# Beacon attention and a max-of-three feed-forward layer on one core: full-height arrays for the first batch's third key tile, the beacon keys and the pairs cast on the chip

## The chip, the cores and the metric

The kernel runs on one core of a Trainium2 chip. The metric is device time in microseconds of one execution. Engines are named as the profile names them: PE is TensorE (matmuls), PEld its weight loads, DVE is VectorE, ACT is ScalarE, POOL is GpSimd, SP is SyncE, which here only issues transfers.

## The reference

Causal attention over 8 batches of 8 heads, with 576 tokens of width 64 and 16 beacon keys and values ahead of them that every token sees; its output, laid out as 4608 tokens by 512, goes through three matrices of 512 by 768, of which the elementwise maximum is taken, and a fourth of 768 by 512.

```python
k_all = np.concatenate([beacon_k, k], axis=2)          # 16 + 576 keys
v_all = np.concatenate([beacon_v, v], axis=2)
scores = scale * np.matmul(q, k_all.transpose(0, 1, 3, 2))
scores = np.where(causal, -1000000000.0, scores)       # beacons are never masked
a = np.exp(scores - scores.max(-1, keepdims=True))
a /= a.sum(-1, keepdims=True) + 1e-09
x = np.matmul(a, v_all)                                # then (B, S, H*D) -> (4608, 512)
h = np.maximum(np.maximum(x @ w1, x @ w2), x @ w3)
return (h @ w_out).astype(np.float32)
```

## The kernel before, in words

Heads are worked in pairs (two heads of 64 fill 128 partitions); four pairs make a batch, two pairs a "quad", 32 pairs in all. For each pair the queries and keys are brought to the layout width by token (`qT`, `kT`), the beacon keys standing ahead of the keys in `kT`, so that there are 592 keys in five tiles of 128, 128, 128, 128 and 80 rows. `emit_scores` (L506) computes scores with keys on the partitions, in four groups per pair, each 64 rows of contraction by 128 columns; ScalarE takes the exponential of a group at once (L532); the triangle is then masked by VectorE (L549, a product with a triangle) or GpSimd (L551). `emit_pv` (L571) multiplies by the values: for a quad and a token half it makes four passes over the key tiles, the first with a block of ones (the sums), the others with the even and odd columns of the values, each matmul 32 columns wide, four of them side by side in the array. `invert_sums` (L606, ScalarE: logarithm and exponential) and `multiply` (L618, VectorE) write the normalized output as `xT`, and the feed-forward units read it: first the three matrices and their maximum (L643 and L666), then the fourth (L685).

Batch 0 is worked in two token halves of 288 (`HALF`), so that the work can begin when half the tokens of a pair have come. In its first half the third key tile holds only 48 keys that any of these tokens sees (`K2`, L97): 16 beacons and 288 tokens less 256. `rows_of` (L99) gives 48 there and the whole tile's rows elsewhere; the value matmuls (L585), the view of the exponentials (L497) and the masks (L542) all go by it. `kT` is set to zero beyond the first half's keys at the start (L151), so the exponentials of the other 80 rows exist.

How the first pairs come in: for pairs 0 and 1, first half, fp32 transfers (`load_half`, L210) are cast on the chip (`cast_half`, L218) into a tile of 96 rows by head, row, width; pairs 2 and 3 and all second halves come cast by the transfer itself (`load_quad`, L226). `turn_half` (L431) turns them on TensorE: for each of the three row groups two transposes of 64 columns, one per head, at column positions 0 and 64. Ahead of each it can put `fill` transposes (L407) of a constant tile. `turn_beacons` (L344) turns the beacon keys: batch 0's with 16 rows, batches 1 to 3 with 48 rows, four transposes each. Later batches' pairs are cast by row, head, width (`cast_piece`, L245) and turned by full transposes of 128 columns (L401), or come back turned from memory.

The order of the work in batch 0 and most of batch 1 is written out by hand, one step after another (`first_steps`, L892 to L1067); each engine takes its instructions in that order. It begins:

```python
("load half", 0, 0, "sp"), ("busy", 17), ("identity",), ("busy", 8), ("triangle",),
...
("half", 0, 0, "ffn", "act", 0, 7),
("cast half", 1, 1, "act"),
("turn keys 0",),
```

"busy" are filler matmuls of 320 columns on the constant tile `busy` (L481), which the third memset from the top of the kernel's code writes on VectorE (L139); the last two numbers of a "half" step are fills ahead of the keys' and of the queries' transposes. The weights of the first layer are loaded by GpSimd's queue at three steps ("load w"), the second of which stands behind the mask of pair 0's second group; w_out is loaded behind a VectorE memset (L332).

Of the kernel before, what the change touches and what calls it, by code (L numbers as in the profile page):

```python
# [8 lines left out]
FP32 = mybir.dt.float32  # L9
BF16 = mybir.dt.bfloat16  # L10
# [6 lines left out]
def kernel(  # L17
# [13 lines left out]
    nc = tc.nc  # L31

    B, H, S, D = q.shape
    Nb = beacon_k.shape[2]
# [13 lines left out]
    QP = S // QR  # L48
    HR = QR // 2
# [160 lines left out]
    def load_half(p, i, queue):  # L210
        st = half_pool.tile([QP, 2, HR, D], FP32, name=f"h32{i}")
        queue.dma_start(
            out=st.rearrange("p h r d -> p h (r d)"),
            in_=half_source(p // PPQ, 0, i, 2 * (p % PPQ), 2),
        )
        stage["half", p, i] = st

    def cast_half(p, i, cast):  # L218
        t16 = half_pool.tile([QP, 2, HR, D], BF16, name=f"h16{i}")
        cast(  # L220
            t16.rearrange("p h r d -> p (h r d)"),
            stage.pop(("half", p, i)).rearrange("p h r d -> p (h r d)"),
        )
        stage["half16", p, 0, i] = t16

    def load_quad(g, h):  # L226
        for i in range(2):
# [115 lines left out]

    def turn_beacons(b0, b1, src):  # L344
        n = Nb * (b1 - b0)
        ps = sc_psum.tile([128, PPB, n], BF16, name="sc")
        for pi in range(PPB):
            nc.tensor.transpose(
                ps[:, pi],
                src[:, 2 * pi : 2 * pi + 2].rearrange("p h d -> p (h d)"),  # L350
                ident[0:n, 0:n],
            )
        if b0 == 0:
            by_act(kTs[0][:, 0:Nb], ps[:, 0, 0:Nb])
        by_act(bT[:, :, Nb * b0 : Nb * b1], ps)
# [48 lines left out]
                ident[0:QP, 0:QP],  # L404
            )

    def fill(ps, n):  # L407
        for i in range(n):
            x0 = 512 + QP * (i % 5)
            for e in range(2):  # L410
                nc.tensor.transpose(
                    ps[64 * e : 64 * e + 64, x0 : x0 + QP],
                    busy[0:QP, 0:64],
                    ident[0:QP, 0:QP],
                    tile_position=(0, 64 * e),
                )

    def keep_turning(n):
        ps = pv_bank(1, [128, 512], FP32)
# [11 lines left out]
    def turn_half(p, h, pv, q_copy=None, idle=0, idle_q=0):  # L431
        for i in range(2):
            src = stage.pop(("half16", p, h, i))
            if pv:
                bank = pv_bank(i, [128, 1024], BF16)
            else:
                bank = ffn_psum.tile([128, 1024], BF16, name="fps")
            ps = bank[:, 0:HALF]

            fill(bank, idle if i == 1 else idle_q)  # L440
            for r in range(HR):
                for e in range(2):
                    nc.tensor.transpose(
                        ps[64 * e : 64 * e + 64, r * QP : (r + 1) * QP],
                        src[:, e, r],
                        ident[0:QP, 0:QP],
                        tile_position=(0, 64 * e),
                    )
# [89 lines left out]
    def emit_masks(p, gi, dve=False):  # L538
        masked.add((p, gi))
        off = 0  # L540
        for t, q0, q1 in groups(p)[gi]:
            n = rows_of(p, t, q1)  # L542
            lo, hi = max(q0, k_tok[t]), min(q1, k_tok[t] + n)
            if lo < hi:
                view = both_heads(p, gi)[0:n, :, off + lo - q0 : off + hi - q0]
                x0 = lo - k_tok[t]
                if dve:
                    m = tri[0:n, None, x0 : x0 + hi - lo]
                    nc.vector.tensor_mul(view, view, m.to_broadcast([n, 2, hi - lo]))  # L549
                else:  # L550
                    nc.gpsimd.affine_select(  # L551
                        out=view,
                        in_=view,
                        compare_op=ALU.is_ge,
                        fill=0.0,
                        base=x0,
                        pattern=[[0, 2], [1, hi - lo]],
                        channel_multiplier=-1,
                    )
            off += q1 - q0  # L560
# [10 lines left out]
    def emit_pv(quad, hf, first=0, last=len(passes), banks=None):  # L571
        b, g = divmod(quad, n_quad)
        v_sb = v_tiles[b]
        for p in range(PPQ * quad, PPQ * (quad + 1)):
            assert all((p, gi) in masked for gi in range(1 if b == 0 and hf == 0 else NG))
        if first == 0:
            banks = banks or [pv_bank(i, [128, 512], FP32) for i in range(2)]
            pv_tiles[quad, hf] = banks
        ps = pv_tiles[quad, hf]
        for part, bank, lo, ca, cb in passes[first:last]:  # L580
            qa, qb = hf * HALF + ca, hf * HALF + cb
            ts = [t for t in range(n_kt) if q_min[t] < qb]
            for t in ts:
                q0 = max(qa, q_min[t])
                n = rows_of(PPQ * quad, t, qb)  # L585
                for j in range(4):
                    lhsT = (
                        ones[0:n]
                        if part == 0
                        else v_sb[0:n, t, head(g, j), part - 1 : D : 2]  # L590
                    )
                    nc.tensor.matmul(  # L592
                        ps[bank][32 * j : 32 * j + 32, lo + q0 - qa : lo + qb - qa],
                        lhsT,
                        at_view(PPQ * quad + j // 2, t, j % 2, q0, qb),
                        start=(t == 0),
                        stop=(t == ts[-1]),
                        tile_position=(0, 32 * j),
                    )
        if last == len(passes):  # L600
            unfinished.append((quad, hf))
# [246 lines left out]
    def widen():  # L848
# [17 lines left out]
        "cast half": lambda p, i, e: cast_half(p, i, by[e]),  # L866
        "cast keys 0": lambda e: by[e](bk16_0, bk32_0),
        "turn keys 0": lambda: turn_beacons(0, 1, bk16_0),
        "half": half,
        "whole": whole,  # L870
# [10 lines left out]
        "cast keys 1": lambda e: by[e](bk16_1, bk32_1),  # L881
        "cast pair": lambda p: cast_pair(p, by_pool, by_pool),
# [5 lines left out]
        "load pair": lambda p, gate="dve": load_pair(p, idle[gate]),  # L888
        "load": next_load,
        "store": lambda: store_y(len(y_out)),  # L890
    }
# [342 lines left out]
```

## Time and profile before

| what | value |
|---|---|
| median of 3 runs | 294.38 us (293.03 to 295.4) |
| profiled execution | 294.65 us, of which span 292.6 us |
| TensorE busy | 281.3 us, 3714 matmuls |
| VectorE, ScalarE, GpSimd busy | 169.6, 150.5, 115.8 us |
| moved by DMA | 49.50 MB, mean 169 GB/s |
| first value pass, first quad (L592) | 44 matmuls, 1.34 us of the chain from 14.60 us |
| first value pass, second quad (L592) | from 18.09 us |
| TensorE's longest waits | 1.3 us for the first memset, 0.7 for w_out, 0.6 for first-layer weights |

A line of a timeline has start and duration in us, engine, line of the kernel, operation, output and inputs by their names, the array shape as rows*columns, the shape of what streams, and how many instructions were merged; in brackets stands the idle time ahead of it and who ended it. The chain is the work that ended last, followed back from the last instruction, in order of time.

### The profile page before, as it was taken

The page shows a single profiled execution, that of the slowest core. Times are in us where ns is not written, and L with a number is a line of the kernel's source. Part 1 is how long each engine was busy: PE and PEld are TensorE (multiplying, and loading weights), DVE is VectorE, ACT ScalarE, POOL GpSimd, SP SyncE. Part 2 cuts the span into 40 slices and gives each one's busy share as a digit, 9 for nine tenths or more (in the row PEclk, how much of TensorE's full clock was granted, in tenths as well). Part 3 has the DMA queues.
Part 4 walks back from the last instruction along what each step waited for, and adds up shares of the span by engine and source line. Part 5 has one row for each costly group of instructions (what it writes and reads, how often), then busy time and mean ns, then how long its engine had stood idle before and what let it go on. Part 6 is the DMA issues. An engine that isn't in the chain of part 4 may idle for free.

```text
span 292.6 us, 8864 instructions
## 1 busy us (share of the span) xinstructions
PE 281.3 (96%) x3714; PEld 160.1 (55%) x3739; DVE 169.6 (58%) x319; ACT 150.5 (51%) x242; POOL 115.8 (40%) x238
## 2 busy tenths in 40 slices
PE   8889999989999999999999999999999999999995
PEld 4656677754454555454545887545454545444442
DVE  1555567837756575566655656565656564474273
ACT  3786576853566676846676256635663552200300
POOL 3618415742546583426454655466323420000000
PEclk9999999999999999999999999999999999999999
DMA  7999979999989999998999899999442003001103
GB/s 131 161 175 185 217 123 225 228 192 261 229 230 256 232 281 270 186 175 263 314 190 181 233 256 268 177 205 214 104 68 98 2 0 137 11 0 74 71 1 143
DMA packets 85111, 49.50 MB, mean 169 GB/s; under 512 B 64208, under 2 KB 79824, under 8 KB 85072
## 3 DMA queue, kind: packets, MB, share of 16 engines
q1 hardware_dynamic: 78864, 43.40, 66.6%
q0 software_dynamic: 5648, 5.21, 11.7%
q8 instruction: 29, 0.48, 0.7%
q10 hardware_dynamic: 560, 0.33, 0.4%
q14 instruction: 10, 0.08, 0.1%
HBM read 35.13 MB, written 14.22 MB: 169 GB/s over the span
## 4 chain that ended last, share of the span: by engine, by line
PE 86%; DMA 7%; POOL 2%; ACT 2%; DVE 1%; issue 1%; POOLq 0%
PE pv L654 21%; PE sc L654 15%; PE wide L654 8%; PE pv L690 6%; PE sc L690 6%; PE sc L517 5%; PE pv L592 4%; DMA w_out_sb<-in_moe_w_out_dram 4%; PE wide L690 3%; PE wide L592 3%; PE sc L592 3%; PE wide L517 3%; DMA w_sb<-in_moe_w_dram 3%; PE pv L481 2%; PE pv L673 1%
## 5 line engine op out<-in xcount | busy, mean ns | idle before, releaser
L532 ACT ACTIVATE at_sb<-sc 128x736 bf16<-128x736 f32 (+5 forms) x91 | 76.5, 867 | 59.3 <-PE sc L517 59.1
L551 POOL TENSOR_SCALAR_AFFINE_SELECT at_sb<-at_sb 128x256 bf16<-128x256 bf16 (+3 forms) x140 | 51.9, 387 | 117.3 <-ACT at_sb L532 117.1
L654 PEld LDWEIGHTS <-w_sb 128*128 128x128 bf16 x648 | 61.1, 98 | 60.4 <-issue 4.7
L654 PE MATMUL pv<-xT,w_sb 128*128 128x512 bf16 (+1 forms) x315 | 65.3, 347 | 0.3
L654 PE MATMUL sc<-xT,w_sb 128*128 128x512 bf16 (+1 forms) x205 | 45.6, 363 | 0.7 <-issue 0.2
L532 ACT ACTIVATE at_sb<-wide 128x736 bf16<-128x736 f32 (+3 forms) x37 | 31.3, 846 | 22.4 <-PE wide L517 22.4
L664 DVE TENSOR_TENSOR hT<-hT,pv 128x512 bf16<-128x512 bf16 x48 | 32.4, 686 | 13.0 <-PE pv L654 13.0
L690 PEld LDWEIGHTS <-hT 128*128 128x128 bf16 x210 | 19.6, 98 | 24.3 <-issue 1.1
L248 POOL CAST p<-st 96x768 bf16<-96x768 f32 x40 | 32.0, 824 | 0.0
L624 DVE TENSOR_TENSOR xT<-pv,recip 128x288 bf16<-128x288 f32 (+2 forms) x48 | 14.2, 350 | 26.7 <-ACT recip L614 26.7
L517 PE MATMUL sc<-qT,kT 64*128 64x288 bf16 (+6 forms) x290 | 27.2, 275 | 2.0 <-POOL at_sb L551 0.6
L664 DVE TENSOR_TENSOR hT<-hT,sc 128x1024 bf16<-128x1024 bf16 (+1 forms) x18 | 19.6, 1098 | 12.7 <-PE sc L654 12.5
L517 PEld LDWEIGHTS <-kT 64*128 64x128 bf16 x400 | 14.9, 94 | 21.8 <-issue 14.7
L592 PEld LDWEIGHTS <-v_sb 128*32 128x32 bf16 (+1 forms) x1408 | 24.7, 96 | 2.6 <-issue 1.3
L654 PE MATMUL wide<-xT,w_sb 128*128 128x512 bf16 (+1 forms) x110 | 24.5, 364 | 0.1
L690 PE MATMUL sc<-w_out_sb,hT 128*128 128x512 bf16 x79 | 19.1, 380 | 1.0 <-DMA w_out_sb<-in_moe_w_out_dram 0.7
L690 PE MATMUL pv<-w_out_sb,hT 128*128 128x512 bf16 x83 | 19.9, 380 | 0.1
L304 POOL CAST v_sb<-st 128x1536 bf16<-128x1536 f32 (+2 forms) x21 | 18.4, 895 | 0.0
L662 DVE CAST hT<-pv 128x512 bf16<-128x512 f32 x20 | 13.7, 688 | 4.8 <-PE pv L654 4.8
L673 PEld LDWEIGHTS <-w_sb 128*128 128x128 bf16 x144 | 13.1, 98 | 3.9 <-issue 1.4
L614 ACT ACTIVATE recip<-lnd 128x288 f32<-128x288 f32 x32 | 14.2, 444 | 1.0
L592 PEld LDWEIGHTS <-ones 128*32 128x32 bf16 (+2 forms) x512 | 11.0, 95 | 6.7 <-issue 4.7
(116 smaller groups left out, 286.3 us busy)
## 6 DMA issues: line engine op xcount, KB each, us to landing
st<-in_q_dram SPq DMA_DIRECT2D x24, 288.0 KB, 5.3
st<-in_k_dram SPq DMA_DIRECT2D x24, 288.0 KB, 5.7
st<-in_v_dram SPq DMA_DIRECT2D x24, 256.0 KB, 5.8
out_dram<-y SPq DMA_DIRECT2D x9, 512.0 KB, 3.3
out_dram<-y SPq DMA_DIRECT2D x17, 256.0 KB, 2.7
w_sb<-in_moe_w_dram POOLq DMA_DIRECT2D x6, 384.0 KB, 7.2
q_dram<-p SPq DMA_DIRECT2D x16, 144.0 KB, 3.1
k_dram<-p SPq DMA_DIRECT2D x16, 144.0 KB, 3.2
```

Source lines behind the costliest of these rows:

```text
L248: cast(t16.rearrange("p r h d -> p h r d"), st[0:QP, i * NQ2 : (i + 1) * NQ2].rearrange("p (h r d) -> p h r d", h=2, r=QR),)
L304: cast(v_sb[0:n, t:t1].rearrange("p t h d -> p (t h d)"), st[0:n, (t - t_lo) * H * D : (t1 - t_lo) * H * D],)
L517: nc.tensor.matmul(ps[:, e, off : off + q1 - q0], kT[hs, 128 * t : 128 * t + 128], qT[hs, q0:q1], start=True, stop=True, tile_position=(64 ...
L532: nc.scalar.activation(out=both_heads(p, gi), in_=ps[:, :, 0 : g_width(p, gi)], func=AF.Exp, scale=scale)
L551: nc.gpsimd.affine_select(out=view, in_=view, compare_op=ALU.is_ge, fill=0.0, base=x0, pattern=[[0, 2], [1, hi - lo]], channel_multiplier=-1,)
L592: nc.tensor.matmul(ps[bank][32 * j : 32 * j + 32, lo + q0 - qa : lo + qb - qa], lhsT, at_view(PPQ * quad + j // 2, t, j % 2, q0, qb), star ...
L614: nc.scalar.activation(out=recip, in_=lnd, func=AF.Exp, scale=-1.0)
L624: nc.vector.tensor_mul(xT[:, 2 * g + part - 1, c0 + ca : c0 + cb], ps[bank][:, lo : lo + cb - ca], recip[:, ca:cb],)
L654: nc.tensor.matmul(dst[:, o0 : o0 + n], w_in[i][:, ct, 128 * (ft + f) : 128 * (ft + f + 1)], xT[:, ct, x0 : x0 + n], start=(ct == 0), stop ...
L664: nc.vector.tensor_max(h, h, ps)
L673: nc.tensor.matmul(ps[:, f], w_in[i][:, ct, 128 * (ft + f) : 128 * (ft + f + 1)], xT[:, ct, tb * TOKB + lo : tb * TOKB + hi], start=(ct == 0),
L690: nc.tensor.matmul(ps[:, t - tt] if two else ps, hT[:, ft, 128 * t : 128 * (t + 1)], w_out_sb[:, ft, :], start=(ft == 0), stop=(ft == n_ft ...
```

## The change

Three things change; the written order of the steps stays as it is.

The function `rows_of` and `K2` go: in batch 0's first half the third key tile is multiplied, viewed and masked with all 128 rows. The beacon tiles `bk16_0` and `bk16_1` get 128 partitions and are set to zero by two memsets on VectorE, which stand ahead of the one for `busy`; their keys are turned by ordinary matmuls with the identity on 128 rows, into an fp32 bank. The casts of pairs 0 and 1, first half, write by row, head, width, and `turn_half` turns such tiles by one full transpose of 128 columns for each row group, with the fills ahead of them in the same form; tiles that come cast by the transfer are turned as before. A way to load half quads on other queues and some defaults of steps are added, and no step of the list uses them.

```diff
-    K2 = Nb + HALF - 256
-
-    def rows_of(p, t, q1):
-        return K2 if p < PPB and t == 2 and q1 <= HALF else k_rows[t]
...
-    bk16_0 = const.tile([Nb, H, D], BF16, name="bk16_0")
+    bk16_0 = const.tile([128, H, D], BF16, name="bk16_0")
+    nc.vector.memset(bk16_0, 0.0)
...
-    bk16_1 = const.tile([NB_PE - Nb, H, D], BF16, name="bk16_1")
+    bk16_1 = const.tile([128, H, D], BF16, name="bk16_1")
+    nc.vector.memset(bk16_1, 0.0)
...
+    def cast_half(p, i, cast, h=0):
+        t16 = half_pool.tile([QP, HR, 2, D], BF16, name=f"h16{i}")
+        cast(t16.rearrange("p r h d -> p h r d"), stage.pop(("half", p, h, i)))
...
-        ps = sc_psum.tile([128, PPB, n], BF16, name="sc")
+        ps = sc_psum.tile([128, PPB, n], FP32, name="sc")
         for pi in range(PPB):
-            nc.tensor.transpose(
+            nc.tensor.matmul(
                 ps[:, pi],
                 src[:, 2 * pi : 2 * pi + 2].rearrange("p h d -> p (h d)"),
-                ident[0:n, 0:n],
+                ident[:, 0:n],
+                start=True,
+                stop=True,
             )
...
+    def turn_column(dst, src, n):
+
+        if len(src.shape) == 2 and src.shape[1] == 128:
+            nc.tensor.transpose(dst, src, ident[0:n, 0:n])
+            return
+        for e in range(2):
+            nc.tensor.transpose(
+                dst[64 * e : 64 * e + 64],
+                src[:, e],
+                ident[0:n, 0:n],
+                tile_position=(0, 64 * e),
+            )
+
+    def fill(ps, n, wide):
+        src = busy[0:QP, 0:128]
         for i in range(n):
             x0 = 512 + QP * (i % 5)
...
+            turn_column(
+                ps[:, x0 : x0 + QP], src if wide else src.rearrange("p (e d) -> p e d", e=2), QP
+            )
...
+            wide = src.shape[1] == HR
+            fill(bank, idle if i == 1 else idle_q, wide)
             for r in range(HR):
...
+                x = src[:, r].rearrange("p h d -> p (h d)") if wide else src[:, :, r]
+                turn_column(ps[:, r * QP : (r + 1) * QP], x, QP)
...
-                    return at[p][0 : rows_of(p, t, q1), off + q0 - lo : off + q1 - lo]
+                    return at[p][0 : k_rows[t], off + q0 - lo : off + q1 - lo]
...
-            n = rows_of(p, t, q1)
+            n = k_rows[t]
...
-                n = rows_of(PPQ * quad, t, qb)
+                n = k_rows[t]
```

More of the change, by code (lines that the diff above doesn't have):

```diff
@@ L215, in load_half, with load_half_quad @@
         )
[L216 to L222, printed above, removed]
-        )
-        stage["half16", p, 0, i] = t16
+        stage["half", p, 0, i] = st
+    def load_half_quad(g, h, i, queue):
+        key = ("half quad", g, h)
+        st = stage[key] if key in stage else new_stage(key)
+        if i == 1:
+            stage.pop(key)
+        st = st[0:QP, i * NQ2 : i * NQ2 + 4 * HR * D].rearrange("p (h r d) -> p h r d", h=4, r=HR)
+        queue.dma_start(
+            out=st.rearrange("p h r d -> p h (r d)"), in_=half_source(g, h, i, 0, 4)
+        )
+        for j in range(PPQ):
+            stage["half", PPQ * g + j, h, i] = st[:, 2 * j : 2 * j + 2]
+    def cast_half(p, i, cast, h=0):
+        t16 = half_pool.tile([QP, HR, 2, D], BF16, name=f"h16{i}")
+        cast(t16.rearrange("p r h d -> p h r d"), stage.pop(("half", p, h, i)))
+        stage["half16", p, h, i] = t16
     def load_quad(g, h):
@@ L438, in turn_half @@
             ps = bank[:, 0:HALF]
-            fill(bank, idle if i == 1 else idle_q)
+            wide = src.shape[1] == HR
+            fill(bank, idle if i == 1 else idle_q, wide)
             for r in range(HR):
[L442 to L448, printed above, removed]
+                x = src[:, r].rearrange("p h d -> p (h d)") if wide else src[:, :, r]
+                turn_column(ps[:, r * QP : (r + 1) * QP], x, QP)
             x0 = i * Nb + HALF * h
@@ L865 @@
         "load v0": load_first_v,
-        "cast half": lambda p, i, e: cast_half(p, i, by[e]),
-        "cast keys 0": lambda e: by[e](bk16_0, bk32_0),
+        "load half quad": lambda g, h, i, e: load_half_quad(g, h, i, queue[e]),
+        "cast half": lambda p, i, e, h=0: cast_half(p, i, by[e], h),
+        "cast keys 0": lambda e: by[e](bk16_0[0:Nb], bk32_0),
         "turn keys 0": lambda: turn_beacons(0, 1, bk16_0),
@@ L880 @@
         "cast v": lambda b, piece: cast_v(b, piece, by_pool),
-        "cast keys 1": lambda e: by[e](bk16_1, bk32_1),
-        "cast pair": lambda p: cast_pair(p, by_pool, by_pool),
+        "cast keys 1": lambda e: by[e](bk16_1[0 : NB_PE - Nb], bk32_1),
+        "cast pair": lambda p, qe="pool", ke="pool": cast_pair(p, by[qe], by[ke]),
         "turn keys 1": lambda: turn_beacons(1, B_PE, bk16_1),
@@ L887 @@
         "load v": lambda b, piece, gate=None: load_v(b, piece, gate and idle[gate]),
-        "load pair": lambda p, gate="dve": load_pair(p, idle[gate]),
+        "load pair": lambda p, gate=None: load_pair(p, gate and idle[gate]),
         "load": next_load,
```

8 lines of the change are left out of this document (removed).

## The prediction

> **What bounds the kernel now.** I read the page first. TensorE is busy 96% of the span, and the chain that ended last is 86% TensorE, so the end is set by the order of TensorE's work plus the few places where it stands still.
>
> ```profile
> span 292.6 us, 8864 instructions
> PE 281.3 (96%) x3714; PEld 160.1 (55%) x3739; DVE 169.6 (58%) x319; ACT 150.5 (51%) x242; POOL 115.8 (40%) x238
> PE 86%; DMA 7%; POOL 2%; ACT 2%; DVE 1%; issue 1%; POOLq 0%
> ```
>
> Then the chain in order of time, from the start to 30 us, since all that the change touches is issued there (columns: start us, us, what). Work on TensorE, ScalarE, VectorE and GpSimd hands on directly to a weight load that TensorE waits for.
>
> ```profile
> 0.95 0.34 DVE busy L139
> 1.33 4.73 PE pv L481 x17
> 6.10 1.57 PE pv L481 x8
> ...
> 14.60 1.34 PE pv L592 x44
> ...
> 18.09 1.30 PE fps L592 x32
> ...
> 19.41 0.42 ACT lnd L612
> ...
> 21.56 0.41 POOL at_sb L551
> 21.96 0.49 POOL w_sb L326
> 22.46 7.48 DMA w_sb<-in_moe_w_dram
> ```
>
> The reader is to see two things: the chain begins with a VectorE memset that the very first matmul waits for, and it passes through both value passes of the first token half (44 matmuls each at L592). Last, the timeline of TensorE around those passes, and around the first value pass of batch 1, which has the same tiles and widths but all 128 rows in its third key tile (three answers, one fence each).
>
> ```profile
> 14.53 0.52 PE L592 MATMUL pv<-at_sb,ones 128*32 128x288 bf16 x12
> 14.97 0.97 PE L592 MATMUL pv<-at_sb,v_sb 128*32 128x288 bf16 x32
> ```
>
> ```profile
> 18.09 0.59 PE L592 MATMUL fps<-at_sb,ones 128*32 128x288 bf16 x12 [0.44 <-DVE at_sb L549]
> 18.61 0.97 PE L592 MATMUL fps<-at_sb,v_sb 128*32 128x288 bf16 x32
> ```
>
> ```profile
> 49.65 0.41 PE L592 MATMUL sc<-at_sb,ones 128*32 128x288 bf16 x12
> 49.89 0.62 PE L592 MATMUL sc<-at_sb,v_sb 128*32 128x288 bf16 x32
> ```
>
> First start to last end is 15.94 - 14.53 = 1.41 us and 19.58 - 18.09 = 1.49 us with 48 rows, and 50.51 - 49.65 = 0.86 us with 128. Nothing else differs between them.
>
> **The change part by part.** The sum is made against the profiled execution, 292.6 us of span and 2.05 around it, 294.65 us; the median of the three runs is 294.38, 0.27 below, and the forecast is put on the median.
>
> *Third key tile with 128 rows.* Each pass goes to the 48-row tile three times and leaves it three times (the last time to the transposes, whose shape differs either way). By the three fences the first quad saves 1.41 - 0.86 = 0.55 us. In the second, what goes on is the logarithm at 19.41, which reads the bank of the sums; it starts before the pass ends at 19.58, so it skips the last switch: of 1.49 - 0.86 = 0.63, the value part (0.97 against 0.62) holds 0.35 for three switches, and a third of that comes off, 0.51. Together -1.06. That one switch costs about 0.1 can be seen elsewhere: the last filler at L481 starts at 7.37 and its follower could start 0.136 later, at 7.51 (the fillers' spacing, below), but the first 64-column transpose starts at 7.60. The masks of 48 partitions become masks of 128 with the same 96 elements on each; VectorE's 80x160 mask takes 228 ns and its 128x160 one 233, so nothing; bounds -0.01 to +0.01 for each of four. No wait is added (the value tile's third part was cast whole before), and no step moves in the written order, so the SP and GpSimd queues keep theirs.
>
> What then is late: between the passes TensorE goes on with transposes, ScalarE and VectorE follow, all waiting for TensorE (ScalarE stood 0.87 us before 16.53, VectorE 2.60 before 16.66), so they move with it. At 19.41 ScalarE itself is free at 18.93 (end of an exponential that moves by the first 0.55); 19.41 - 1.06 = 18.35 lies just under 18.93 - 0.55 = 18.38. So 0.03 is lost: -1.03.
>
> *Two memsets.* They come first on VectorE, ahead of the busy memset. The zero memsets of bf16 at L150 and L151 show as uint32, 24 elements in 78 ns and 40 in 92, 0.875 ns an element; 512 bf16 are 256 of these, 78 + 232 x 0.875 = 281 ns. The next memset starts 45 ns before one ends (0.95 + 0.325 against 1.23), so 0.24 us each, +0.47 for both. As 512 bf16 elements at the busy memset's rate (320 in 325 ns) they would be 0.44 each, +0.88, the other end. VectorE's later memsets shift too, covered by its 3.96 us of idle before 5.76. TensorE's first matmul goes from 1.33 to 1.80, and the 25 fillers behind it.
>
> Not all of that arrives at 7.60. The page's clock row is 9 all through, but the fillers are not equal: 17 start in 4.73 us, 0.278 each; of the last eight, the final three start 0.135 apart (0.57 for three that take 0.30 each). With 0.27 and 0.136 the eight fit 1.27 us between first and last start if the rate doubles at about 6.75. If it doubles at that time whatever TensorE's start, 0.47 us of fillers at the slow rate are made up at the fast one, and half arrives: +0.24. If it doubles a fixed time after the start, all arrives: +0.47. I take 0.24 and keep both. [...] The trace bears out the doubling near 6.75, and cannot show the phase of another execution.
>
> *Pairs 0 and 1, first half, by full transposes.* Two halves run side by side: at L443 six pairs take 0.42 us with 0.21 of it the last one's own, so 0.042 from pair to pair; at L401 twelve full ones take 0.68, (0.68 - 0.21) / 11 = 0.043 each. So half as many instructions save nothing: 0, bounds -0.05 and +0.05 for 27 of them. But the fillers, the transposes and the beacon matmuls now have one array shape: the switch at 7.60 goes, -0.10, in the chain. The two about the beacon keys (8.28 and 8.71) go too, but TensorE waits there for ScalarE's qT copy anyway ([0.18 <-ACT qT L451] at 8.71), so 0. Without that cover they would be worth -0.2.
>
> *Casts and beacons.* The casts now write rows head by head, runs of 64. ScalarE's copy at L451 writes interleaved and takes 399 ns for 288 elements, its straight logarithm 416, so nothing on ScalarE, where two of the three casts lie in the chain before 8.26; if strided cost 10%, +0.05 on the one in the chain. VectorE's one cast (356 ns at 5.76) has 2.16 us of idle behind it; without it, +0.1. Four beacon matmuls on 128 rows take what 16 rows did (at L592 48 rows by 48 columns take 193 ns, 128 by 80 take 199: columns count, not rows), between -0.05 and +0.1, and lie in ScalarE's cover until 8.97; their fp32 bank is read by ScalarE at 168 to 216 ns now, 16 to 64 columns, the 288 fp32 columns of the logarithm at 416 fit the same line, so 0. The second beacon turn at 28.68 follows scores of 64 rows and precedes full matmuls: before, the switch came behind it, after, ahead of it: 0.
>
> *Sum.* -1.03 + 0.24 - 0.10 = -0.89 at 19.41. From there the chain is ScalarE, GpSimd's mask, its weight issue at 21.96, and 7.48 us of transfer. Does the transfer move too? DMA by half microseconds:
>
> ```profile
> 22.00:22.50 0.50, 0.50 (x7) 0.46 (x5) 0.20 (x1) 0.16 (x1) 0.50 (x2) 1.00 0.49 106
> 22.50:23.00 0.50, 0.50 (x6) 0.32 (x4) 0.50 (x2) 0.00 (x0) 0.50 (x1) 1.00 0.43 99
> ```
>
> The last two columns are the DMA share and GB/s. From 22.0 to 23.0, ahead of the weights, the engines are half free (and the weights' own share begins at 23, after 1.0 us of start), so an issue 0.89 earlier finds room. The next transfer on the chain (output weights, 50.77 to 63.14) is issued by steps that follow TensorE, after a stretch with a DMA share of 0.03 (42 to 44 us), so no backlog holds it. The whole -0.89 reaches the end: 293.76 for the profiled execution, 293.5 for the median.
>
> **The rivals.** *The transfer eats it.* If the first-layer weights land at 29.94 whatever the issue, TensorE's wait for them (0.59 before 29.98, by the timeline) grows by 0.89 and the time is 294.4. For it: shares over 1 from 23 to 30 us. Against: the half-free engines ahead.
>
> [...]
>
> *More is gained.* If the clock doubles earlier than here, the fillers end before ScalarE's cast does (7.41), the memsets cost nothing, and the two switches at the beacon keys may count: -1.03 - 0.10 - 0.2 = -1.33, 293.05. Against: at 8.71 TensorE waits for ScalarE.
>
> **How the numbers follow.** Forecast 0.56, eaten 0.20, late clock 0.12, more gained 0.12. The forecast's own range, with the memsets at 0.47 to 0.88 of cost, the casts and the masks: 293.1 to 294.2. The three runs shown spread from 293.03 to 295.4, so a median of a few runs moves by about 0.7; range 292.4 to 295.0, which takes in all but the far ends of the rivals. One per cent, 2.9 us, is about what a measurement of this kernel can tell from no change: faster than 291.4 needs three times the whole term sum, 0.05; slower than 297.3 needs the late clock twice, 0.03; within, 0.92.
>
> **What would show it.** In the profile after: each of the two value passes at about 0.86 to 0.95 us from first start to last end, with no weight load of 48 rows; the first filler at 1.80; no gap of 0.09 at the first transposes; the first-layer weights issued near 21.1 and TensorE's wait for them still about 0.6. It is wrong if the passes stay at 1.4 (then rows are not what costs), if the wait for the weights grows to 1.5 (eaten), or if the fillers are still at 0.27 us after 8 us (late clock).

## The result and the profile after

The changed kernel took 296.2 us (median of 20 runs, 293.85 to 300.15) against 293.78 (20 runs, 292.85 to 295.4): ratio 1.0071, 95% interval 1.0052 to 1.009. It is 2.4 us slower, where 0.9 faster was forecast. The profiled execution took 297.46 us with a span of 295.6, against 294.65 and 292.6, so 3.0 us more in the span; this difference is taken apart below.

The page, the same lines as before:

```profile
span 295.6 us, 8807 instructions
...
PE 281.8 (95%) x3684; PEld 160.7 (54%) x3709; DVE 171.2 (58%) x321; ACT 150.3 (51%) x242; POOL 115.7 (39%) x238
...
PEclk9999999989999999999999999999999999999999
...
q8 instruction: 29, 0.48, 0.7%
...
PE 93%; DVE 3%; issue 2%; ACT 1%; DVEq 0%
```

TensorE does 30 matmuls fewer and is busy about as long. New are one 8 in the row of the granted clock and the 2% of "issue" in the chain: time in which TensorE waited for nothing that the profile shows. The fourth line, which the page of before has word for word too, will matter: one queue carried 29 packets, 0.48 MB, with the program itself.

The chain in order of time (start us, us, what), with the parts that the change touches and the first thing that nobody had forecast:

```profile
0.94 0.27 DVE bk L128
1.22 0.27 DVE bk L131
1.50 0.34 DVE busy L136
...
39.10 1.61 issue
...
56.38 1.84 issue
```

TensorE's timeline at the two value passes:

```profile
15.11 0.40 PE L606 MATMUL pv<-at_sb,ones 128*32 128x288 bf16 x12
15.35 0.62 PE L606 MATMUL pv<-at_sb,v_sb 128*32 128x288 bf16 x32
...
18.12 0.53 PE L606 MATMUL fps<-at_sb,ones 128*32 128x288 bf16 x12 [0.45 <-DVE at_sb L563]
18.47 0.63 PE L606 MATMUL fps<-at_sb,v_sb 128*32 128x288 bf16 x32
...
20.83 1.91 PE L687 MATMUL fps<-xT,w_sb 128*128 128x256 bf16 x16 [0.23 <-DVE xT L638]
```

The passes take 15.97 - 15.11 = 0.86 us and 19.10 - 18.12 = 0.98, where they took 1.41 and 1.49: the part of the change that was to save time does. Even so the first group of 16 matmuls at L687 starts at 20.83, only 0.40 earlier than before (21.23). From there I compared the same instruction in both traces:

| instruction | before | after | after minus before |
|---|---|---|---|
| first filler | 1.33 | 1.89 | +0.56 |
| first transpose | 7.60 | 7.96 | +0.36 |
| scores ahead of the first value pass | 14.20 | 14.79 | +0.59 |
| first group of L687 | 21.23 | 20.83 | -0.40 |
| group of L687 before the first stop | 37.69 | 36.89 | -0.80 |
| group of L687 behind the first stop | 40.58 | 41.38 | +0.80 |
| value pass from 54.97 | 54.17 | 54.97 | +0.80 |
| first matmul of the output weights | 63.18 | 65.84 | +2.66 |
| span | 292.6 | 295.6 | +3.0 |

Between 21 and 37 us it got better still: TensorE's wait of 0.59 us for the first-layer weights is not there any more. Then the gain is lost in two places. The timeline of TensorE around each of them, first before (the two places, and the one stop of this kind that it has), then after:

```profile
39.62 0.60 PE L517 MATMUL sc<-qT,kT 64*128 64x288 bf16 x8
...
54.67 1.18 PE L592 MATMUL sc<-at_sb,v_sb 128*32 128x288 bf16 x56
...
56.03 0.68 PE L401 MATMUL wide<-ident,p 96*128 96x96 bf16 x12
56.55 1.91 PE L673 MATMUL pv<-xT,w_sb 128*128 128x256 bf16 x16
...
60.63 0.29 PE L592 MATMUL pv<-at_sb,v_sb 128*32 128x80 bf16 x12 [0.56 <-issue]
```

```profile
38.81 0.29 PE L531 MATMUL sc<-qT,kT 64*128 64x288 bf16 x1
40.71 0.50 PE L531 MATMUL sc<-qT,kT 64*128 64x288 bf16 x6 [1.61 <-issue]
```

```profile
55.47 0.91 PE L606 MATMUL sc<-at_sb,v_sb 128*32 128x288 bf16 x29
58.22 0.74 PE L606 MATMUL sc<-at_sb,v_sb 128*32 128x192 bf16 x27 [1.84 <-issue]
...
59.29 1.14 PE L409 MATMUL wide<-ident,p 96*128 96x96 bf16 x12
60.23 2.66 PE L687 MATMUL pv<-xT,w_sb 128*128 128x256 bf16 x16
```

TensorE stops in the middle of a group whose inputs are all there: behind one of eight score matmuls, and behind 29 of 56 value matmuls. No semaphore ends the wait; the profile can only write "issue". The second stop has a second price, shown by stretches of 2 us (columns: us, busy time and count of PE, PEld, DVE, ACT, POOL, granted clock, DMA share, GB/s):

```profile
56.00:58.00 2.00, 0.38 (x21) 0.15 (x9) 0.95 (x7) 0.59 (x1) 0.98 (x3) 1.00 1.31 168
58.00:60.00 2.00, 1.78 (x39) 1.36 (x40) 0.00 (x0) 0.96 (x3) 0.00 (x0) 0.59 1.24 199
60.00:62.00 2.00, 2.00 (x16) 1.51 (x14) 1.53 (x4) 1.15 (x2) 0.41 (x1) 0.56 1.21 195
62.00:64.00 2.00, 2.00 (x47) 1.37 (x48) 1.40 (x3) 0.74 (x2) 0.00 (x0) 1.00 1.21 238
```

Behind it the clock was halved from 58.35 to 61.76 us: the 12 transposes take 1.14 instead of 0.68, the 16 matmuls 2.66 instead of 1.91, 1.21 us in all. With +0.80 before it, +1.84, +1.21, less a stop of 0.56 and a wait of 0.73 for the output weights that before had in this stretch, that makes +2.56 of the measured +2.66.

So the question was what stops TensorE. I counted its weight loads and matmuls in the order of the program: 7478 before, 7418 after, 60 fewer (30 transposes, 18 of them fills, each with its weight load). The pages have the half of it, 3739 and 3709 weight loads; the expectations below give two more for every kernel, which changes none of the differences. The stops after stand ahead of numbers 1213 and 1725; the one stop of before, 0.56 us at 60.07, ahead of number 1981. All three are 189 plus a multiple of 256. And 29 such numbers lie in either program (189 to 189 + 28 x 256 = 7357), as many as the queue of the program has packets, each of 16,384 bytes in the trace. In the trace the packet for the block that starts at 1213 comes after TensorE has passed 957, at 33.14, one block earlier. Its record lies between 37.96 and 39.40 us, 4.8 after that; TensorE goes on at 40.71. The same for 1725: 1469 passed at 50.81, packet from 55.44 to 56.70, TensorE on at 58.22. The DMA view of after for the time between passing and packet, and for the packet (queue, kind: packets, MB, share of 16 engines; two answers):

```profile
q1 hardware_dynamic: 1102, 1.05, 112.7%
q14 instruction: 1, 0.01, 1.0%
```

```profile
q1 hardware_dynamic: 547, 0.31, 108.8%
q8 instruction: 1, 0.02, 5.6%
```

From 50.8 to 55.4 us the engines carry loads at a share of 1.13 and nothing of q8; from 55.4 to 56.8 the packet is there. Before, the number 957 was passed at 32.27, the packet lay from 33.71 to 34.69, only 1.4 us behind, and nothing stopped.

Two things make this sharper. TensorE's records also hold instructions that only handle semaphores, four up to 21.2 us and fifteen more between 120 and 237 us, which the count above leaves out. With them counted, every stop of kind "issue" of over 0.3 us, in the traces of all fifteen runs in this document, stands ahead of the same place modulo 256. And in each of these stops TensorE goes on 1.27 to 1.66 us after the end of the latest packet (at 40.71, 1.31 after 39.40; at 58.22, 1.52 after 56.70).

**Theory A**: the change took 60 instructions out ahead of this stretch, so every edge between two fetched blocks moved 60 places on in the code, onto work that uses a block up in little time (the blocks followed here, with value passes and transposes, last 5.0 to 6.0 us) while its successor is late among the loads. The work itself is not slower. **The rivals**: the stops come from the altered forms themselves (full transposes, more rows), or from work that now meets the loads at another time, wherever the edges are; then the place of the stop would not follow the count of instructions. In the expectations A is the first of these.

By A, kernels with equal counts modulo 256 stop at the same instruction, whatever else they do. Fillers are the means: matmuls whose result nobody reads, 17 and then 8 of 320 columns in the first microseconds. Cut into more and narrower ones of about the same total columns, they move the edges of all that follows and take nothing away. A "pair" below is one weight load and its matmul, so two instructions.

### The profile page after: what moved, and what is told of

Its sections match the earlier page's. It is cut to its first block, busy times and chain, and to the rows that moved or that the text cites. A ratio compares the mean times of both kernels' runs of the same rounds, so it can differ in the third digit from the quotient of the medians.

```text
span 295.6 us, 8807 instructions
## 1 busy us (share of the span) xinstructions
PE 281.8 (95%) x3684; PEld 160.7 (54%) x3709; DVE 171.2 (58%) x321; ACT 150.3 (51%) x242; POOL 115.7 (39%) x238
## 4 chain that ended last, share of the span: by engine, by line
PE 93%; DVE 3%; issue 2%; ACT 1%; DVEq 0%
PE pv L668 21%; PE sc L668 15%; PE wide L668 8%; PE sc L531 7%; PE pv L704 6%; PE sc L704 6%; PE pv L606 5%; PE sc L606 5%; PE wide L704 3%; PE wide L606 3%; PE wide L531 3%; PE pv L687 2%; PE pv L495 2%; PE fps L687 2%; PE sc L687 1%
## 5 line engine op out<-in xcount | busy, mean ns | idle before, releaser
L687 PEld LDWEIGHTS <-w_sb 128*128 128x128 bf16 x144 | 13.5, 100 | 3.6 <-issue 1.4
L606 PEld LDWEIGHTS <-ones 128*32 128x32 bf16 (+1 forms) x512 | 11.0, 95 | 6.8 <-issue 4.6
```

The lines of the kernel that those rows point to most:

```text
L606: nc.tensor.matmul(ps[bank][32 * j : 32 * j + 32, lo + q0 - qa : lo + qb - qa], lhsT, at_view(PPQ * quad + j // 2, t, j % 2, q0, qb), star ...
L687: nc.tensor.matmul(ps[:, f], w_in[i][:, ct, 128 * (ft + f) : 128 * (ft + f + 1)], xT[:, ct, tb * TOKB + lo : tb * TOKB + hi], start=(ct == 0),
```

## The experiments

**1. The rows alone.** Before, with the third key tile at 128 rows and nothing else; 7478 instructions, edges as before.

```diff
-        return K2 if p < PPB and t == 2 and q1 <= HALF else k_rows[t]
+        return k_rows[t]
```

> Only the third key tile's 128 rows, on the kernel before; TensorE's count of instructions stays 7480. Theory A (the loss of the changed kernel lies in where the 256-instruction blocks of TensorE's program end, 60 instructions having gone): the two value passes shrink from 1.4 to about 0.9 us each and the edges stand where they stood before, so the first feed-forward matmul comes 0.9 to 1.0 us earlier and the time is 0.5 to 1.0 us below the kernel before. Rival B (the 128-row passes bring the loss, by more work for the masks or by the array): 1 to 2.5 us above the kernel before.

293.02 us (12 runs) against 293.93: ratio 0.9967, interval 0.9947 to 0.9987. The passes in its timeline:

```profile
14.24 0.40 PE L590 MATMUL pv<-at_sb,ones 128*32 128x288 bf16 x12
14.47 0.62 PE L590 MATMUL pv<-at_sb,v_sb 128*32 128x288 bf16 x32
...
17.25 0.53 PE L590 MATMUL fps<-at_sb,ones 128*32 128x288 bf16 x12 [0.45 <-DVE at_sb L547]
17.59 0.63 PE L590 MATMUL fps<-at_sb,v_sb 128*32 128x288 bf16 x32
```

0.85 and 0.97 us. At the end 0.9 us arrive, where this part was forecast to give 1.03, and TensorE still waits for the first-layer weights (two of its waits):

```profile
PE fps L671 <- DMA w_sb<-in_moe_w_dram: 0.7, 1, 0.7
...
PE pv L590 <- issue: 0.2, 1, 0.2
```

**2. After, with the edges of before.** 30 pairs added to the fillers at about the same columns: 7478 instructions.

```diff
-        ("busy", 17),
+        ("busy", 37, 145),
...
-        ("busy", 8),
+        ("busy", 18, 145),
```

> The changed kernel, with its 25 fillers of 320 columns cut into 55 of 145 columns: the same columns streamed, 30 pairs of weight load and matmul more, so that TensorE's program is 7480 instructions long as before and every block of 256 ends at the place in the code where it ended in the kernel before. Theory A: the stops of 1.6 and 1.8 us in the middle of the score and value matmuls (39 and 56 us) go, none over about 0.6 is left, the clock stays at 1.00, and the time is 0.2 to 0.7 us below the kernel before. Rival B (the loss is in the new array forms, the memsets or the transfers that they move): the stops stay, wherever the blocks end, and the time stays 2 to 2.5 us above the kernel before.

293.5 us (12 runs), ratio 0.9977, interval 0.9956 to 0.9998, beside the same runs of before as experiment 1. All of the change is in it and it is 2.7 us below the median of after (0.94% by the two ratios to before). The score matmuls are one group of eight again, and the only long stop left is that of before, of 0.6 us ahead of number 1981 (timeline, waits):

```profile
38.40 0.60 PE L531 MATMUL sc<-qT,kT 64*128 64x288 bf16 x8
```

```profile
PE pv L606 <- issue: 0.6, 1, 0.6
```

**3. Before, with the edges of after.** 98 pairs added: 7674 = 7418 + 256 instructions. Nothing of the change is in it.

```diff
-        ("busy", 17),
+        ("busy", 84, 65),
...
-        ("busy", 8),
+        ("busy", 39, 65),
```

> The kernel before with none of the change; its 25 fillers of 320 columns are cut into 123 of 65, which adds 98 pairs, 196 instructions, so that the blocks of 256 end at the places in the code where they end in the changed kernel (60 fewer, 196 more: the same place in a block). Theory A: it stops for 1 to 2 us at the same two places as the changed kernel (the third scores of pair 5 and the value pass of quad 1, batch 0's second or batch 1's first half, whichever stands there), and is 1.5 to 3.5 us slower than the kernel before. Rival B: it stays within 0.5 us of the kernel before.

296.53 us (7 runs), ratio 1.0063, interval 1.0031 to 1.0095: the kernel before, slowed as much as the change slowed it (1.0071). And the stops come behind the very same matmuls, one of eight and 29 of 56, and at the next edge (timeline, two answers):

```profile
39.09 0.29 PE L517 MATMUL sc<-qT,kT 64*128 64x288 bf16 x1
39.95 0.51 PE L517 MATMUL sc<-qT,kT 64*128 64x288 bf16 x6 [0.58 <-issue]
```

```profile
54.72 0.91 PE L592 MATMUL sc<-at_sb,v_sb 128*32 128x288 bf16 x29
56.35 0.52 PE L592 MATMUL sc<-at_sb,v_sb 128*32 128x192 bf16 x27 [0.72 <-issue]
...
61.02 0.65 PE L592 MATMUL sc<-at_sb,ones 128*32 128x288 bf16 x17
62.82 0.22 PE L592 MATMUL sc<-at_sb,ones 80*32 80x80 bf16 x3 [1.14 <-issue]
```

The two stops are shorter than the 1 to 2 us expected, and the rest of the loss lies at later edges. The rivals cannot have this: no altered form of the change is in this kernel. A new rival is the form of the fillers, 65 columns each; experiment 4 has it in part. No run has fillers this narrow at the edges of before, but after itself is slow with fillers of 320, and the four longest stops of this trace, all at edges (the fourth 0.48 us, at 126.42), make 2.9 us against 0.56 before.

**4. The control.** After, with 128 pairs added: one whole block, so the edges stay where after has them. It tells whether the fillers' new form, and not the edges, had helped in experiment 2.

```diff
-        ("busy", 17),
+        ("busy", 104, 52),
...
-        ("busy", 8),
+        ("busy", 49, 52),
```

> The changed kernel with its fillers cut into 153 of 52 columns: 128 pairs, 256 instructions, exactly one block more, so that the blocks end at the same places in the code as in the changed kernel itself. It is the control for the kernel with 30 pairs more: if finer fillers alone did the good (by the clock's start or otherwise), it would be as fast as that one. Theory A: the two stops stay and it is 1.5 to 3 us slower than the kernel before, like the changed kernel. Rival C (it is the finer fillers that help): below the kernel before by 0.2 to 0.7.

296.79 us (6 runs), ratio 1.0092, interval 1.0063 to 1.012. Added pairs do not help; the edges do. Its three stops, each ahead of a number at 189 modulo 256, all lie at places where experiment 3 stops too: two are shown below, the third (1.4 us) is at 126.4. The stop at 56, which was expected to stay, is not in this profile:

```profile
39.97 0.51 PE L531 MATMUL sc<-qT,kT 64*128 64x288 bf16 x6 [0.89 <-issue]
```

```profile
61.75 0.22 PE L606 MATMUL sc<-at_sb,ones 80*32 80x80 bf16 x3 [1.04 <-issue]
```

**5. Another place for the edges, forecast from A.** Before, with 64 pairs: 7606, the edges half a block from those of before.

```diff
-        ("busy", 17),
+        ("busy", 61, 90),
...
-        ("busy", 8),
+        ("busy", 28, 90),
```

> The kernel before with none of the change; its 25 fillers of 320 columns are cut into 89 of 90 columns, 64 pairs more, so that the blocks of 256 instructions end half a block away. By the profile of before, the block that then starts at 79.4 us (the two value passes of batch 1's second quad and what stands around them) is used up in 2.8 us, and its follower is fetched, going by the fetches near there (3.4 to 5.0 us from an edge to the end of the fetch, and 1.3 to 1.5 more until TensorE goes on), after 4.7 to 6.5. Theory A: a stop of 1.5 to 3.5 us at 81 to 84 us, where neither kernel has stopped so far; the time 1 to 3.5 us above the kernel before. Rival D (only the two places seen so far are touchy, for a reason of their own): no new stop there, within 0.7 us of the kernel before.

297.24 us (9 runs), ratio 1.009, interval 1.0055 to 1.0126: the slowing came. The place did not: its profiled execution, at 295.38 us among its faster ones, stops at 20.4 and 62.25, both at edges, and only for 0.34 us at 82.98, where I had expected the main one; there the packet came 0.63 us after the edge before was passed. The same kernel was profiled once more.

> The kernel before with 64 pairs more, one more look: its median is 3.4 us above the kernel before, but the profiled execution was one of its fastest (295.38) and stopped only 0.34 us at 83. Theory A as worked out: in an execution near the median a stop of 1 to 3.5 us stands at 81 to 85 us. If not, its loss is at the other edges (20 and 61 us), longer there than 0.7 and 0.8.

296.42 us, beside 294.04 for before; its stops of kind "issue" are again at L443 (20.89) and L592 (63.7), and there is none at 83 (waits of TensorE):

```profile
PE pv L443 <- issue: 1.3, 1, 1.3
...
PE sc L592 <- issue: 0.3, 1, 0.3
```

The stop of 1.3 us at 20.89 is followed by half clock from 23.16 to 26.58. So which places can stop TensorE follows from the count; which of them do, and how long, differs from one execution to the next.

**6. The same for after.** A second profile of the unaltered kernel.

> The changed kernel once more, one look, for a second execution's profile: its times spread from 293.85 to 300.15, those of the kernel before from 292.85 to 295.4. Theory A: stops stand again at edges of 256 instructions (39 to 41 us and 55 to 61 us), with lengths that differ from the first profile's 1.6 and 1.8 us, since the fetch competes with transfers; whether TensorE's clock halves for a stretch depends on a stop's length. Rival: the stops stand elsewhere, off the edges.

299.06 us, beside 294.04. It stops at three edges, 1.4 us near 62, 1.3 at 127.69, 1.7 at 177.7, and not at 39. The last stands ahead of number 5047, 183 modulo 256, six places ahead of the edge; six semaphore instructions of TensorE lie between 122 and 159 us, and with them counted it is at the edge. It also waits 1.8 us for keys, with half clock from 25.12 to 28.54. So half clock does not go by a stop's length alone: it came behind the 1.3 us at 20.89 in before_64_again and not behind the 1.7 us here. The runs of after reach from 293.85 to 300.15, which fits executions that each have their own stops out of one set of places; two of them are profiled.

**7. A load issued later.** Not the edges but the fetch: in after, the load of batch 1's first three value tiles (768 KB, issued by SyncE behind a memset on GpSimd) is written behind a step of scores. By A the packet for 1213 then comes sooner.

```diff
-        ("load v", 1, 0, "pool"),
...
         ("scores", 4, 3, 0),
+        ("load v", 1, 0, "pool"),
```

> The changed kernel with one step moved: the load of batch 1's first three value tiles, 768 KB, comes after the scores at about 41 us instead of at 29, where the transfer engines then have little to do. The blocks of TensorE's program stand as in the changed kernel. It asks why the block's fetch comes late at 38 us. If the crowd of transfers holds it (Theory A), the fetch that began 4.8 us after its edge begins sooner, the stop of 1.6 us at 39 shrinks under 0.8, while the one at 56 us stays or grows, as the load now lies nearer to it; time 0.3 to 1.5 us below the changed kernel. If the fetch takes as long without the crowd, the stop at 39 stays at 1.3 to 1.8.

295.32 us (10 runs), ratio 1.0047, interval 1.002 to 1.0073. The move is smaller than the expectation says: the first of these transfers is issued at 32.25 us instead of 30.11, not at 41, and that is still ahead of the edge. The packet now lies at 34.69 to 35.74, 2.0 us after 957 was passed at 32.66 instead of 4.8, and the stop at 39 is gone, with the same number of instructions as after. The stop at 56, which was expected to stay or grow, is not there either; a later edge has one of 1.42 us (timeline, two answers):

```profile
38.30 0.60 PE L531 MATMUL sc<-qT,kT 64*128 64x288 bf16 x8
```

```profile
61.10 0.22 PE L606 MATMUL sc<-at_sb,ones 80*32 80x80 bf16 x3 [1.42 <-issue]
```

An earlier packet and no stop go together here, as A has it. That the moved load did it is not shown: after_again, with nothing moved, has no stop at 39 either (957 passed at 35.16, packet from 38.25, 3.1 us behind), and the interval overlaps that of after (1.0052 to 1.009).

**8. The memsets, and other edges.** After_30pairs with the two memsets of zeros moved behind VectorE's other ones at the start; then the same with 44 pairs (7506).

```diff
-    nc.vector.memset(bk16_0, 0.0)
-    nc.vector.memset(bk16_1, 0.0)
...
     nc.vector.memset(ones, 1.0)
+    nc.vector.memset(bk16_0, 0.0)
+    nc.vector.memset(bk16_1, 0.0)
```

> The changed kernel with 30 pairs more (as in the run of that name) and with the two zero memsets moved behind the memsets of the kernel before, so that the first filler starts at 1.33 us again. It measures the start's term of the prediction by itself. If the memsets cost 0.2 to 0.5 at the start, it is 0.2 to 0.5 us below the changed kernel with 30 pairs, so 0.6 to 1.2 below the kernel before; if their cost is hidden, equal to it.

> The same with 14 pairs more still (fillers of 116 columns). In the trace of the kernel with the rows alone, edges 28 instructions earlier leave no block of the crowded stretch under 5.4 us, where the shortest is 4.9 now. Theory A: no stop over 0.3 us in the trace, and 0 to 0.6 us below the kernel with 30 pairs, the fastest of all. Otherwise equal to it, and a stop stays.

293.21 us (12 runs), ratio 0.9966, interval 0.9939 to 0.9992; and 292.99 (12 runs), 0.9966, 0.9945 to 0.9988. The memsets cost perhaps 0.3 us at the end (293.5 in experiment 2 against 293.21, each beside its own runs of before, intervals overlapping). The kernels with 30 and with 44 pairs cannot be told apart. With 44 pairs this trace shows no stop of kind "issue" in TensorE's waits; among what is left are the start and the two weight loads:

```profile
PE pv L495 <- DVE busy L134: 1.3, 1, 1.3
...
PE fps L687 <- DMA w_sb<-in_moe_w_dram: 0.5, 1, 0.5
PE sc L704 <- DMA w_out_sb<-in_moe_w_out_dram: 0.4, 1, 0.4
```

**9. Are the full transposes and the beacon matmuls worth anything?** Rows alone, with 14 pairs: 7506 again, so the edges of late_zero_44pairs in a kernel without the other two parts.

```diff
-        return K2 if p < PPB and t == 2 and q1 <= HALF else k_rows[t]
+        return k_rows[t]
...
-        ("busy", 17),
+        ("busy", 26, 205),
...
-        ("busy", 8),
+        ("busy", 13, 205),
```

> The kernel before with the 128 rows and 14 pairs more: fillers cut into 39 of 205 columns. It has the edges of the kernel with the zero memsets late and 44 pairs, but none of the full transposes, the beacon matmuls and the memsets. If those two parts bring nothing (the prediction gave -0.1 for the switch that goes), both are equal within 0.3 us and no stop over 0.3 stands in the trace; if they bring 0.5 or more, it is that much slower.

293.92 us (12 runs), ratio 0.9988, interval 0.9965 to 1.0011, so 0.9 above late_zero_44pairs, which was not expected; its trace has a stop of 0.7 us at an edge at 142.4. The two had not run side by side, so they were timed again together.

> The kernel with the rows alone and 14 pairs more, timed on the same chip as the next one. If the other two parts of the change (full transposes and beacon matmuls, with the memsets out of the way) bring nothing, both are equal within 0.4 us; if the 0.6 us between their earlier ratios to the kernel before (0.9988 and 0.9966) is theirs, this one is again 0.4 to 0.9 us slower than the next.

> The changed kernel with late zero memsets and 44 pairs more, beside the one with the rows alone at the same edges: equal within 0.4 us, or 0.4 to 0.9 us faster, as said there; below the kernel before by 0.5 to 1.3 in either case.

292.67 us (12 runs; ratio 0.9959, 0.9934 to 0.9984) and 292.85 (12 runs; 0.9958, 0.9941 to 0.9974): no difference, so the 0.9 was not borne out. Both profiles have a stop at the edge at 1981 (0.74 and 0.41 us), so the edges of 44 pairs are not free of stops in every execution. At equal edges and with the memsets out of the way, full transposes and beacon matmuls bring nothing that these runs can tell. Rows of 128 bring about 0.9 us at the edges of before (experiment 1); the 1.2 us or more below before in this last pair have other edges in them too.

## Why the prediction was wrong

*What bounds the kernel*: right as far as it went. TensorE's order sets the end, with the few places where it stands still. But the page of before had such a place that I passed over: a wait of 0.6 us of kind "issue" at L592, and "issue 1%" in the chain that I quoted. It stands at an edge, 1.41 us after the end of a packet: the same mechanism, mildly.

*Third key tile, -1.03*: right. Passes of 0.86 and 0.98 us; experiment 1 has 0.9 us less at the end with this part alone.

*Two memsets, +0.24*: too small in this execution. Each took 0.27 as forecast, the first filler came +0.56 late (forecast +0.47), and +0.36 of it reached the first transpose (forecast +0.14 with the switch). The spacing of the fillers halved at about 7.15 us, against 6.8 before: the doubling that the forecast had held at 6.75 came later here. Then VectorE's steps ahead of the first pass stretched, three masks 1.49 instead of 1.40 and a cast 0.62 instead of 0.41, and the scores started +0.59 late. So -0.40 at 20.83 where -0.89 had been forecast for 19.41. Experiment 8 puts the memsets at about 0.3 in the time, with overlapping intervals, near the forecast. With the fillers cut into 55, they ended at about the same time whether they began at 1.34 or 1.88 (first transpose at 7.26 and at 7.23), as the rate doubled at about 6.2 in the one execution and 5.3 in the other. So what the memsets cost at the start is in part a matter of luck in each execution. That the rate doubles at the same time whatever TensorE's start, on which the 0.24 rests, no run shows, nor that it doubles a fixed time after the start: it came at about 6.8 us in before, 7.15 in after, 6.2 in late_zero_30pairs and 5.3 in after_30pairs, which is 5.5, 5.3, 4.9 and 3.4 us after the first filler.

*The rivals*: none was it. The transfer did not eat the gain; the wait for the first-layer weights went from 0.59 to nothing, against the forecast of 0.6: they were issued 0.37 earlier (21.54 against 21.91) and the transfer that TensorE waited for took 7.04 us instead of 7.48, so it landed 0.81 earlier, while TensorE came to its group only 0.11 earlier (28.89 against 29.00). The forecast had let the issue move and not the length, which is 7.24 to 7.80 us in three other traces (late_zero_44pairs, rows_only, after_again), so this part was luck. The late clock, 0.12 among the chances, did not come at the start: the fillers' spacing halved at about 7.15 us, ahead of the first transpose at 7.96. Half clock did come at 58.35, behind a stop, where nothing in the forecast had it.

*The step that failed*: "So half as many instructions save nothing: 0, bounds -0.05 and +0.05 for 27 of them." As durations that was right (experiment 9), though 30 pairs went and not 27: 12 transposes and 18 fills. But I took instructions for nothing but their durations. Thirty pairs fewer move all edges between fetched blocks by 60 places, and that was worth 2.7 us: 296.2 for after, 293.5 for after with the edges of before. The sentence "from there ... the whole -0.89 reaches the end" has the same hole, since it rests on before's stops staying where and as long as they were. My range ended at 295.0, and its bounds came from the steps I had listed, none of which could move something at 39 or 56 us.

*Still open*: what holds the fetch back. The latest fetches lie in crowded stretches, but crowding alone does not tell: in experiment 5 an edge in a crowded stretch had its packet only 0.63 us after the edge before was passed, and in after the packet came 0.35 us behind an edge passed at 203.2, where the DMA share is 0.96 (200 to 206 us), much as the 0.43 behind the one passed at 232.5, where it is 0.01 (230 to 236). The delay at one edge differs between executions of one kernel too, 4.8 and 3.1 us for 957 in after. I did not find a rule by which to forecast the length of a stop, only the places.

## What to carry to other kernels

Before you cost an edit that changes the number of instructions of a long program, count them: find the stops of kind "issue" in the trace before, see whether their places are equal modulo 256 (the engine's semaphore instructions counted), and look at what the edges will move onto. To tell such a shift from the edit's own worth, pad the changed kernel back to the old count with harmless instructions (here 30 narrow fillers) and compare that; the effect of this edit with the old edges, -0.23% (interval -0.44% to -0.02%, some 0.7 us), was hidden under a shift of 2.7 us. What is then left to win is had by choosing the padding, though no run shows an edge set that is free of stops in every execution, and, as with every effect of this size, only runs made side by side decide.

## What the runs showed of the hardware

TensorE's program came in 29 packets of 16,384 bytes for 7418 as for 7478 weight loads and matmuls, and in 30 for 7674 (both such kernels). In after, up to 85 us, a packet began 0.5 to 4.8 us after TensorE had passed into the block ahead of it (later on some began up to 3.8 us before), and late ones cost up to 1.84 us of standstill. That a packet holds 256 instructions is my estimate, from the places of the stops, equal modulo 256, and from the number of packets. No profile here shows more than three stops of over 0.5 us at its 29 or 30 edges, so most edges cost less than that, but the others made this kernel 0.7% slower.

A stop can also cost clock. Behind the one of 1.84 us in after the granted clock was 0.50 for 3.41 us (58.35 to 61.76), worth 1.21 us; behind the one of 1.61 us it stayed at 1.00. The clock's record in this trace begins at 7.15 us, where the fillers' spacing halves, with 51.20 us at 1.00, then 3.41 at 0.50 and 235.52 at 1.00: 15, 1 and 69 steps of 3.413 us. In before it begins at 6.79 with 286.72 us at 1.00, 84 such steps. The two other halved stretches, 25.12 to 28.54 (after_again) and 23.16 to 26.58 (before_64_again), are as long as one step. Of after, the steps around the two stops (columns as above):

```profile
37.87:41.28 3.41, 1.80 (x19) 1.14 (x17) 1.53 (x3) 0.58 (x2) 0.00 (x0) 1.00 1.06 162
54.94:58.35 3.41, 1.57 (x62) 1.21 (x62) 2.01 (x8) 1.65 (x2) 1.88 (x6) 1.00 1.26 202
```

TensorE was busy for 1.80 us of the first, and the clock stayed; for 1.57 of the second, and behind it the clock was halved. In the 3.41 us ahead of the other two halvings it was busy for 1.62 us (after_again) and 1.72 (before_64_again). So in these three TensorE was busy for 46 to 50% of the step before the clock was lost. Busy time alone does not decide it: in two other steps, counted off in the same way, TensorE was busy for 1.69 us (after_again, 175.31 to 178.72) and 1.70 (before_64pairs, 61.07 to 64.48), and the clock stayed, as it did in after behind 290.45 to 293.87, with 1.70 us.

A value pass of 44 matmuls that goes to a tile of 48 rows and back takes 1.41 us, one on 128 rows throughout 0.86: 0.55 for the five switches inside it, by estimate 0.11 us each.
